# Four groups of VectorE instructions moved past the start of the next step in a fused state-space and mixture kernel

## The chip, the cores and the metric

The kernel runs on one core of a Trainium2 chip, in 32-bit floats throughout. The metric is the device time of one execution in microseconds (us).

## The reference, cut to what matters

A Mamba-2 state-space block is followed by a mixture of four experts, each a two-layer network on 3072 tokens of width 256:

```python
for c in range(S // 32):                       # per head, over chunks
    M = (C_c @ B_c.T) * L                      # L: causal decays
    y[c] = M @ x_c + (C_c @ state) * decay_to_i
    state = decay_full * state + (B_c * decay_from_j).T @ x_c
x = y.transpose(0, 2, 1, 3).reshape(3072, 256)
p = domain_probs / (domain_probs.sum(-1, keepdims=True) + 1e-9)
for e in range(4):                             # width 256 -> 1024 -> 256
    h = np.maximum(x @ w1[e], 0.0)
    out += p[:, e:e+1] * (h @ w2[e])
```

## The kernel before, in words

The tokens are cut into 24 chunks of 128. Six blocks (k = 0 to 5) of four chunks, 512 tokens each, go through the experts. For each block the experts' hidden width is cut into eight steps (r = 0 to 7, two for each expert), so there are 48 steps, n = 8k + r. Steps 0 and 1 are done in a plain way ahead of the loop; steps 2 to 47 are the loop of L718.

A step multiplies by Strassen's scheme in Winograd's form: seven products where eight would be needed, with sums before and after. A *first-layer product* i (`fmul(n, i)`, L436) is four matmuls of 256 columns; it writes or adds to one of two PSUM banks, X (products 1, 6, 7, 4) or Y (products 2, 5, 3). Products 1, 2 and 5 begin their bank anew, so product 5 may start only when the old Y has been read. ScalarE copies X after products 1, 6 and 7 (`snap`, L443), and VectorE adds the copy to Y (`total`, L448): the sums z11, z22, z12. From these, and from X directly, VectorE makes the gated activations h11, h22, h12, h21 (`gated`, L458), and from them four differences (`diff`, L465):

    T3 = h22 - h12,  T1 = h12 - h11,  T2 = h22 - T1,  T4 = h21 - T2

The seven *second-layer products* (`smul`, L521) of step n take these as their moving operand and are run inside step n+1, between that step's first-layer products. TensorE's order in the body of step n is: product 1, product 2, second-layer 1 of step n-1, product 6, second-layer 3, the attention outputs (`outputs`, L376 and L382, in some steps), products 5 and 7, second-layer 7 and 5, products 3 and 4, second-layer 6 (reads T2), 2, the scores of a chunk (`scores`, L353, in some steps), second-layer 4 (reads T4).

VectorE's order in the body of step n is: z11, h11, the first half of a chunk's decays (`decay_part`, a scan, L330), the transpose of the last block's output (`turned_out`, L610, where r = 1), z22, h22, the second half of the decays, z12, h21, h12, the masking of the scores (L363), T3, a short scan (L313), T1, T2, T4, the end of the last block's combination and the state updates.

The chunk of a later block enters (`c_in`) in steps with r = 0, 2, 4, 6 and leaves through `outputs` (`c_out`) in steps with r = 1, 3, 5, 7 of blocks 1 to 4; block 0 has r = 2, 4, 6 and 2, 3, 5, 7, and the last block has neither. After `outputs`, VectorE turns the chunk's contribution to the state, adds the decayed old state and spreads it for the next use (`carry`, L399, L401, L406). The state is used again one block later.

At the first step of a block (`ending`, r = 0) the four accumulators of the block before are combined into its output: part 0 on VectorE (L541), part 1 on GpSimd (four adds, L544 to L547), part 2 on VectorE (L549, L550, in block 0 L552 too).

All instructions are issued in the order in which the program states them, each engine running its own in that order; waits between engines are added where data or buffers need them. T2 and T4 have two buffers each, z three, the accumulators one each.

The end of the loop body, where the change is, is L793 to L801; its start is L732 to L737:

```python
        opened(n)                    # product 1, snap, product 2
        total(n, 1, "11")
        gated(n, "11", "z11")
        if c_in is not None:
            masks(c_in)
            decay_part(c_in, 0)
```

Of the kernel before, what the change touches and what calls it, by code (L numbers as in the profile page):

```python
# [17 lines left out]
def kernel(  # L18
# [101 lines left out]
    def load_chunk(c):  # L120
        load_tokens(c)
        load_decays(c, nc.sync)
# [3 lines left out]
    def load_w1(n):  # L126
        e, jj = divmod(n % SPB, JJ)
        t1 = wt1[n] = wts.tile([P, 7, HB], FP32, tag="wt1", name="wt1", bufs=5)
        if n >= SPB:
            nc.sync.dma_start(out=t1, in_=w1_d[n % SPB])  # L130
            return
        for k in range(2):
            nc.sync.dma_start(
                out=t1[:, 2 * k:2 * k + 2],
                in_=w1[e, k * P:k * P + P].rearrange("p (a f) -> p a f", a=2)[
                    :, :, jj * HB:jj * HB + HB])

    def load_w2(n):
        e, jj = divmod(n % SPB, JJ)
        t2 = wt2[n] = wts.tile([P, 7 * HB], FP32, tag="wt2", name="wt2", bufs=5)  # L140
        if n >= SPB:
            nc.sync.dma_start(out=t2, in_=w2_d[n % SPB])
            return
        for i in range(2):
            f = i * FH + jj * HB
            nc.sync.dma_start(
                out=t2[:, i * 2 * HB:(i + 1) * 2 * HB].rearrange("p (j m) -> p j m", j=JJ),
                in_=w2[e, f:f + HB].rearrange("(j p) m -> p j m", p=P))
# [17 lines left out]
    def sum_w1(n, part=None):  # L166


        if n < SPB:
            sums_of(lambda w: wt1[n][:, w].rearrange("p (j m) -> p j m", j=JJ), part)  # L170
            if part != 0:
                nc.gpsimd.dma_start(out=w1_d[n], in_=wt1[n])

    def sum_w2(n, part=None):
        if n < SPB:
            sums_of(lambda w: w2_op(n, w), part)
            if part != 0:
                nc.gpsimd.dma_start(out=w2_d[n], in_=wt2[n])
# [92 lines left out]
    def load_gate(k, e):  # L271
        g = gate[k, e] = ffn.tile([P, CPB, P], FP32, tag="gate", name="gate", bufs=3)
        nc.sync.dma_start(out=g, in_=p_d.rearrange(
            "(i k) e s -> k e i s", k=NBLK)[k, e].partition_broadcast(P))
# [64 lines left out]
    def masks(c):  # L339

        s = st[c]
        m = s["ctm"] = att.tile([HN, NT, P], FP32, tag="ctm", name="ctm")
        for t in range(NT):
            nc.scalar.mul(m[:, t], s["xb"][:, OCT:OCT + P], tmask[:, t:t + 1])
# [48 lines left out]
    def carry(c):  # L393
        s = st.pop(c)
        if "A" not in s:
            return

        S = att.tile([HN, D], FP32, tag="S", name="S", bufs=6)
        nc.vector.transpose(S, s["A"].rearrange("p t n -> p (t n)"))  # L399
        if c >= CPB:  # L400
            nc.vector.scalar_tensor_tensor(  # L401
                out=S, in0=state[c % CPB][0], scalar=s["dec"][:, P - 1:P], in1=S,
                op0=ALU.mult, op1=ALU.add)

        M = att.tile([HN, NQ, D], FP32, tag="M", name="M", bufs=6)
        nc.vector.tensor_mul(M, S.unsqueeze(1).to_broadcast([HN, NQ, D]), qmask)  # L406
        state[c % CPB] = S, M
# [37 lines left out]
    def total(n, i, b):  # L445

        z = first[n]["z" + b] = ffn.tile([P, JJ, HB], FP32, tag="z", name="z", bufs=3)
        nc.vector.tensor_add(z, first[n]["Y"], first[n][i])  # L448

    def gated(n, b, src):  # L450

        if n not in hid:
            hid[n] = {}
        h = hid[n][b] = ffn.tile([P, JJ, HB], FP32, tag="h" + b, name="h" + b)
        k, e = n // SPB, n % SPB // JJ
        half = int(b[1]) - 1
        g = gate[k, e].rearrange("p c s -> p (c s)")[:, half * HB:half * HB + HB]
        nc.vector.scalar_tensor_tensor(  # L458
            out=h, in0=first[n][src], scalar=0.0, in1=g.unsqueeze(1).to_broadcast([P, JJ, HB]),
            op0=ALU.max, op1=ALU.mult)  # L460

    def diff(n, o, x, y):
        h = hid[n]
        h[o] = ffn.tile([P, JJ, HB], FP32, tag="h" + o, name="h" + o)
        nc.vector.tensor_sub(h[o], h[x], h[y])  # L465
# [66 lines left out]
    def combine(k, part):  # L532

        p1, p3 = kept[k, 0][:, 0], kept[k, 0][:, 1]
        if part == 0:
            kept[k, "o"] = ffn.tile([P, 2, BLK], FP32, tag="o", name="o", bufs=1)
            kept[k, "u"] = ffn.tile([P, 3, HB], FP32, tag="u", name="u", bufs=1)
        o, u = kept[k, "o"], kept[k, "u"]
        b1, b2 = slice(0, HB), slice(HB, BLK)
        if part == 0:  # L540
            nc.vector.tensor_add(u[:, 0], acc[k, 2][:, 0], p1)  # L541
        if part == 1:
            p7, p5 = kept[k, 1][:, 0], kept[k, 1][:, 1]
            nc.gpsimd.tensor_add(u[:, 1], u[:, 0], p7)  # L544
            nc.gpsimd.tensor_add(u[:, 2], u[:, 0], p5)
            nc.gpsimd.tensor_add(o[:, 1, b2], u[:, 1], p5)
            nc.gpsimd.tensor_add(o[:, 0, b2], u[:, 2], p3)  # L547
        if part == 2:
            nc.vector.tensor_add(o[:, 0, b1], acc[k, 2][:, 1], p1)  # L549
            nc.vector.tensor_add(o[:, 1, b1], acc[k, 3][:, 0], u[:, 1])  # L550
            if k == 0 and PLAIN:
                nc.vector.tensor_add(o[:, 1, b2], acc[k, 3][:, 1], o[:, 1, b2])  # L552
# [69 lines left out]
    def opened(n):  # L622

        fmul(n, 1)
        snap(n, 1)
        fmul(n, 2)
# [88 lines left out]
    carry(1)  # L715


    for n in range(PLAIN, NS):  # L718
        k, r = divmod(n, SPB)

        enter, exit = ({2: 1, 4: 2, 6: 3}, {2: 0, 3: 1, 5: 2, 7: 3}) if k == 0 else (
            {0: 0, 2: 1, 4: 2, 6: 3}, {1: 0, 3: 1, 5: 2, 7: 3})
        c_in, c_out = (CPB * (k + 1) + d[r] if r in d and k < NBLK - 1 else None
                       for d in (enter, exit))
        ending = r == 0 and k > 0
        e = r // JJ
        if r % JJ == 0 and n + JJ < NS:
            load_gate(*divmod(n // JJ + 1, E))
        if PLAIN + 2 < n + 2 < NS:
            load_w1(n + 2)  # L730
            load_w2(n + 2)
        opened(n)  # L732
        total(n, 1, "11")
        gated(n, "11", "z11")
        if c_in is not None:
            masks(c_in)
            decay_part(c_in, 0)  # L737
        if n == PLAIN:
            for m in range(PLAIN):
                sum_w1(m, 1)  # L740
        elif n == PLAIN + 1:
            for m in range(1, PLAIN):
                sum_w2(m, 1)
        sum_w1(n + 2)
        if n > PLAIN:
            sum_w2(n + 1)
        if r == 1 and k > 0:
            turned_out(k - 1)
        if k > 0 and 1 <= r <= CPB:
            leave(k - 1, r - 1)  # L750
        smul(n - 1, 1)
        fmul(n, 6)
        snap(n, 6)
        smul(n - 1, 3)
        if ending:
            keep(k - 1, 0)
        if c_out is not None:
            outputs(c_out, ps_att, "att")
        fmul(n, 5)
        fmul(n, 7)  # L760
        snap(n, 7)
        total(n, 7, "22")
        smul(n - 1, 7)
        smul(n - 1, 5)
        if ending:
            keep(k - 1, 1)
        gated(n, "22", "z22")
        if c_in is not None:
            decay_part(c_in, 1)
        if n == PLAIN:  # L770
            sum_w2(0, 1)
        if c_out is not None and c_out + 2 < NCH:
            load_chunk(c_out + 2)
        fmul(n, 3)
        total(n, 6, "12")
        fmul(n, 4)
        gated(n, "21", "X")
        gated(n, "12", "z12")
        if r == SPB - 1 and k < NBLK - 1:
            sums(k + 1)  # L780
        smul(n - 1, 6)
        smul(n - 1, 2)
        if c_in is not None:
            scores(c_in, ((ps_att, "att"), (ps_att, "att"), (ps_f, "X"), (ps_f, "Y")))
            masked(c_in, (2, 3, 0, 1))
        diff(n, "T3", "22", "12")
        if c_in is not None:
            decay_part(c_in, 2)
        if ending:
            combine(k - 1, 0)  # L790
            combine(k - 1, 1)
        smul(n - 1, 4)
        diff(n, "T1", "12", "11")  # L793
        diff(n, "T2", "22", "T1")
        diff(n, "T4", "21", "T2")
        if ending:
            combine(k - 1, 2)
        if PLAIN < n <= CPB:
            carry(n - 1)
        if c_out is not None:  # L800
            carry(c_out)  # L801
    finish(NS - 1)


# [43 lines left out]
```

## Time and profile before

| | |
|---|---|
| time, median of three runs | 664.32 us (663.93 to 665.34) |
| the profiled execution's own time | 664.32 us |
| its span, first to last instruction | 662.5 us |
| TensorE matmul busy | 646.7 us, 98% |
| VectorE busy | 496.7 us, 75% |
| ScalarE, GpSimd busy | 115.0 us, 113.0 us (17% each) |
| mean granted TensorE clock | 0.999 of full speed |
| chain that ended last | TensorE 87%, VectorE 7%, DMA 4%, issue 1% |

Times are in microseconds from the first instruction. PE is TensorE's matmul stream, PEld its weight loads, which overlap it; DVE is VectorE, ACT ScalarE, POOL GpSimd, SP the engine that issues most transfers. In a row of the timeline the columns are start, duration, engine, line, operation, output and inputs; the bracket at the end is the time for which the engine stood idle before it and what released it. Several instructions of one kind in a row are merged into one with a count. Matmuls overlap one another in the pipeline: four of them are shown as 1.03 us, but follow each other group by group every 0.86 us.

### The profile page before, as it was taken

The page shows a single profiled execution, that of the slowest core. Times are in us where ns is not written, and L with a number is a line of the kernel's source. Part 1 is how long each engine was busy: PE and PEld are TensorE (multiplying, and loading weights), DVE is VectorE, ACT ScalarE, POOL GpSimd, SP SyncE. Part 2 cuts the span into 40 slices and gives each one's busy share as a digit, 9 for nine tenths or more (in the row PEclk, how much of TensorE's full clock was granted, in tenths as well). Part 3 has the DMA queues.
Part 4 walks back from the last instruction along what each step waited for, and adds up shares of the span by engine and source line. Part 5 has one row for each costly group of instructions (what it writes and reads, how often), then busy time and mean ns, then how long its engine had stood idle before and what let it go on. Part 6 is the DMA issues. An engine that isn't in the chain of part 4 may idle for free.

```text
span 662.5 us, 8905 instructions
## 1 busy us (share of the span) xinstructions
PE 646.7 (98%) x3359; PEld 541.2 (82%) x3359; DVE 496.7 (75%) x814; ACT 115.0 (17%) x246; POOL 113.0 (17%) x157
## 2 busy tenths in 40 slices
PE   8899989999999999999999999999999999999997
PEld 5687878878888887888887888888788888888886
DVE  8678788787786788767878777678867776856655
ACT  3011111221112122111122121112111112111110
POOL 4867483030000002000003000000200000200000
PEclk9999999999999999999999999999999999999999
DMA  7998998405669512868730566841265851176000
GB/s 228 318 335 326 344 371 312 171 2 171 207 257 330 186 56 65 251 192 290 279 131 3 195 208 255 323 169 56 75 242 191 307 220 62 19 244 242 5 1 32
DMA packets 68666, 127.09 MB, mean 192 GB/s; under 512 B 26616, under 2 KB 50576, under 8 KB 68624
## 3 DMA queue, kind: packets, MB, share of 16 engines
q1 hardware_dynamic: 65568, 111.32, 48.7%
q0 software_dynamic: 2304, 14.68, 5.4%
q8 instruction: 26, 0.43, 0.3%
q10 hardware_dynamic: 752, 0.54, 0.3%
q14 instruction: 16, 0.13, 0.1%
HBM read 108.44 MB, written 18.07 MB: 191 GB/s over the span
## 4 chain that ended last, share of the span: by engine, by line
PE 87%; DVE 7%; DMA 4%; issue 1%; SPq 0%; POOL 0%; ACT 0%; DVEq 0%; ACTq 0%; POOLq 0%
PE acc L521 40%; PE X L436 22%; PE Y L436 18%; DVE hT L465 3%; PE g L353 2%; PE acc L502 2%; PE y L382 1%; DVE MT L363 1%; DMA gate<-p_d 1%; PE y L376 1%; DMA ac_d<-a_sb 1%; DMA p_d<-p_sb 1%; DMA xb<-in_xbc_dram 1%; DVE z L448 1%; DMA wt<-w_d 1%
## 5 line engine op out<-in xcount | busy, mean ns | idle before, releaser
L521 PE MATMUL acc<-hT,wt 128*128 128x256 f32 x736 | 183.1, 382 | 0.0
L448 DVE TENSOR_TENSOR z<-Y,snap 128x512 f32<-128x512 f32 x138 | 94.6, 686 | 117.6 <-ACT snap L443 99.5
L443 ACT COPY snap<-X 128x512 f32<-128x512 f32 x138 | 80.8, 585 | 474.8 <-PE X L436 472.8
L521 PEld LDWEIGHTS acc<-hT,wt 128*128 128x128 f32 x736 | 138.3, 190 | 24.0 <-issue 6.0
L436 PE MATMUL X<-yS,wt 128*128 128x256 f32 x552 | 141.7, 379 | 0.0
L521 PE MATMUL acc<-h,wt 128*128 128x256 f32 x552 | 141.5, 379 | 0.0
L521 PEld LDWEIGHTS acc<-h,wt 128*128 128x128 f32 x552 | 104.9, 190 | 14.3
L436 PEld LDWEIGHTS X<-yS,wt 128*128 128x128 f32 x552 | 104.9, 190 | 14.3
L458 DVE SCALAR_TENSOR_TENSOR h<-z,gate 128x512 f32<-128x512 f32 x138 | 98.1, 711 | 3.5 <-PE acc L502 0.4
L436 PE MATMUL Y<-yT,wt 128*128 128x256 f32 x368 | 94.4, 379 | 0.0
L465 DVE TENSOR_TENSOR hT<-h,hT 128x512 f32<-128x512 f32 x92 | 75.8, 823 | 3.2
L436 PEld LDWEIGHTS Y<-yT,wt 128*128 128x128 f32 x368 | 68.8, 190 | 10.6
L465 DVE TENSOR_TENSOR hT<-h,h 128x512 f32<-128x512 f32 x92 | 64.4, 723 | 0.8
L436 PE MATMUL Y<-yS,wt 128*128 128x256 f32 x184 | 49.8, 393 | 6.8 <-DVE z L448 6.8
L330 DVE TENSOR_TENSOR_SCAN LT<-ab,ident 128x512 f32<-128x512 f32 x42 | 53.6, 1279 | 0.7 <-POOL wt L161 0.7
L335 POOL TENSOR_TENSOR MT<-xb,LT 128x128 f32<-128x128 f32 x20 | 8.5, 427 | 251.9 <-PE Y L436 133.8
L436 PE MATMUL X<-yT,wt 128*128 128x256 f32 x184 | 47.2, 379 | 0.0
L363 DVE TENSOR_TENSOR MT<-g,LT 128x256 f32<-128x256 f32 x96 | 34.0, 417 | 17.3 <-PE g L353 17.3
L436 PEld LDWEIGHTS Y<-yS,wt 128*128 128x128 f32 x184 | 32.9, 189 | 16.8 <-DVE z L448 10.3
L316 POOL TENSOR_TENSOR cts<-ctm,dec 128x256 f32<-128x256 f32 x20 | 18.5, 924 | 161.2 <-ACT snap L443 158.3
L458 DVE SCALAR_TENSOR_TENSOR h<-X,gate 128x512 f32<-128x512 f32 x50 | 34.3, 687 | 10.8 <-PE X L436 4.6
L436 PEld LDWEIGHTS X<-yT,wt 128*128 128x128 f32 x184 | 35.0, 190 | 4.8
(91 smaller groups left out, 340.3 us busy)
## 6 DMA issues: line engine op xcount, KB each, us to landing
wt<-w_d SPq DMA_DIRECT2D x80, 896.0 KB, 10.5
w_d<-wt POOLq DMA_DIRECT2D x16, 896.0 KB, 6.8
ab<-acut_d SPq DMA_DIRECT2D x21, 512.0 KB, 5.5
wt<-in_w_dram SPq DMA_DIRECT2D x32, 256.0 KB, 7.0
xb<-in_xbc_dram SPq DMA_DIRECT2D x24, 320.0 KB, 3.6
gate<-p_d SPq DMA_DIRECT2D x24, 256.0 KB, 9.3
out_dram<-ot SPq DMA_DIRECT2D x160, 16.0 KB, 5.0
ah<-ac_d SPq DMA_DIRECT2D x20, 64.0 KB
```

Of the source, the lines that this page charges most:

```text
L316: nc.gpsimd.tensor_mul(cts, s["ctm"], dec.unsqueeze(1).to_broadcast([HN, NT, P]))
L330: nc.vector.tensor_tensor_scan(out=LT[:, i * w:i * w + w], data0=s["a"][i], data1=ident.rearrange("p h s -> p (h s)")[:, :w], initial=0.0, ...
L335: nc.gpsimd.tensor_mul(s["MT"][:, :, P:], s["xb"][:, OB:OB + HN].rearrange("p (h n) -> p h n", h=NH), s["LT"][:, :, P - 1:P].to_broadcast( ...
L353: nc.tensor.matmul(out=g.rearrange("p t s -> p (t s)"), lhsT=s["xb"][k, OBT:OBT + P], rhs=s["ctm"][k].rearrange("p t s -> p (t s)"), start ...
L363: nc.vector.tensor_mul(s["MT"][:, h, 0:P], s["g"][q], s["LT"][:, h])
L436: nc.tensor.matmul(out=f[bank][:, j], lhsT=wt1[n][:, w, j * P:j * P + P], rhs=rhs, start=(i in (1, 2, 5) and j == 0), stop=(j == JJ - 1), ...
L443: nc.scalar.copy(out=s, in_=first[n]["X"])
L448: nc.vector.tensor_add(z, first[n]["Y"], first[n][i])
L458: nc.vector.scalar_tensor_tensor(out=h, in0=first[n][src], scalar=0.0, in1=g.unsqueeze(1).to_broadcast([P, JJ, HB]), op0=ALU.max, op1=ALU. ...
L465: nc.vector.tensor_sub(h[o], h[x], h[y])
L502: nc.tensor.matmul(out=acc[k, u][:, half], lhsT=w2_op(n, w)[:, j], rhs=hid[n][f"{i + 1}{b}"][:, j], start=(begins and i == 0 and j == 0), ...
L521: nc.tensor.matmul(out=acc[k, u][:, half], lhsT=w2_op(n, w)[:, j], rhs=rhs[:, j], start=(begins and j == 0), stop=(n % SPB == SPB - 1 and ...
```

## The change

At the end of a step, the differences T2 and T4, part 2 of the combination and the state updates are no longer issued. They are kept in a list, and the list is issued in the next step behind its z11 and h11 and ahead of its decays. After the last step the list is issued ahead of the final part.

```diff
+    late = []
     for n in range(PLAIN, NS):
...
         opened(n)
         total(n, 1, "11")
         gated(n, "11", "z11")
+        for work in late:
+            work()
         if c_in is not None:
             masks(c_in)
             decay_part(c_in, 0)
...
         smul(n - 1, 4)
         diff(n, "T1", "12", "11")
-        diff(n, "T2", "22", "T1")
-        diff(n, "T4", "21", "T2")
+        late = [lambda n=n: diff(n, "T2", "22", "T1"), lambda n=n: diff(n, "T4", "21", "T2")]
         if ending:
-            combine(k - 1, 2)
+            late.append(lambda k=k: combine(k - 1, 2))
         if PLAIN < n <= CPB:
-            carry(n - 1)
+            late.append(lambda n=n: carry(n - 1))
         if c_out is not None:
-            carry(c_out)
+            late.append(lambda c=c_out: carry(c))
+    for work in late:
+        work()
     finish(NS - 1)
```

## The prediction, made before the changed kernel ran

> **What bounds the kernel now.** I read the page first: busy times, then the costliest groups with the idle time in front of them.
>
> ```profile
> PE 646.7 (98%) x3359; PEld 541.2 (82%) x3359; DVE 496.7 (75%) x814; ACT 115.0 (17%) x246; POOL 113.0 (17%) x157
> L436 PE MATMUL Y<-yS,wt 128*128 128x256 f32 x184 | 49.8, 393 | 6.8 <-DVE z L448 6.8
> ```
>
> TensorE is busy for 646.7 of 662.5 us, so a change that leaves its work alone can only win idle time or lose more. Of the 15.8 us idle, 6.8 stand before one group, the matmuls that refill bank Y from yS: first-layer product 5. They wait for VectorE's z (L448), the sum z11, which must have read the old Y. The list of waits says "7 times, longest 1.4". The timeline gives the seven places: steps n=3 (0.65), 5 (1.24), 6 (0.43) and 9, 17, 25, 33 (1.37, 1.01, 1.01, 1.07). The timeline of both engines at the start of step 17, parts left out, shows what holds z11:
>
> ```profile
> 249.95 1.21 DVE L465 TENSOR_TENSOR hT<-h,h 128x512 f32<-128x512 f32 x1
> 251.19 2.23 DVE L465 TENSOR_TENSOR hT<-h,hT 128x512 f32<-128x512 f32 x2
> ...
> 253.03 0.70 PE L382 MATMUL y<-MT,xb 128*32 128x144 f32 x16
> ...
> 253.34 0.41 DVE L549 TENSOR_TENSOR o<-acc,kept 128x256 f32<-128x256 f32 x1
> 253.68 0.41 DVE L550 TENSOR_TENSOR o<-acc,u 128x256 f32<-128x256 f32 x1
> ...
> 254.01 0.68 DVE L448 TENSOR_TENSOR z<-Y,snap 128x512 f32<-128x512 f32 x1
> ...
> 254.72 0.69 DVE L458 SCALAR_TENSOR_TENSOR h<-z,gate 128x512 f32<-128x512 f32 x1
> ...
> 254.74 1.13 PE L436 MATMUL Y<-yS,wt 128*128 128x256 f32 x4 [1.01 <-DVE z L448]
> ...
> 255.33 1.24 DVE L610 STREAM_TRANSPOSE ot<-o 128x1024 f32<-128x1024 f32 x1
> ...
> 257.39 0.69 DVE L448 TENSOR_TENSOR z<-Y,snap 128x512 f32<-128x512 f32 x1 [0.82 <-ACT snap L443]
> ...
> 258.30 1.03 PE L436 MATMUL Y<-yT,wt 128*128 128x256 f32 x4
> ```
>
> VectorE never idles from T1 (249.95) to the output transpose: T2, T4 and the two combining adds stand ahead of z11, and nobody needs them so early (the second-layer products that read T2 and T4 come at the end of the step). The last two rows are the second thing to see. The next sum, z22 (257.39), is waited for by product 3 (258.30): z22 ends at 258.08, its weight load starts at once. So **z22 has no slack towards TensorE, and what VectorE has before it is a cushion of 0.82 us** (its idle time before z22). The moved instructions land exactly there. The question is thus in each step: gain at z11 against cushion at z22. An ordinary even step, n=18:
>
> ```profile
> 262.88 1.42 DVE L465 TENSOR_TENSOR hT<-h,hT 128x512 f32<-128x512 f32 x2
> ...
> 263.48 1.03 PE L436 MATMUL Y<-yT,wt 128*128 128x256 f32 x4
> ...
> 264.21 0.20 DVE L399 STREAM_TRANSPOSE S<-A 128x32 f32<-128x32 f32 x1
> ...
> 264.95 0.69 DVE L448 TENSOR_TENSOR z<-Y,snap 128x512 f32<-128x512 f32 x1
> ...
> 265.67 0.69 DVE L458 SCALAR_TENSOR_TENSOR h<-z,gate 128x512 f32<-128x512 f32 x1
> ...
> 266.28 1.22 DVE L330 TENSOR_TENSOR_SCAN LT<-ab,ident 128x512 f32<-128x512 f32 x1
> ...
> 269.47 0.69 DVE L448 TENSOR_TENSOR z<-Y,snap 128x512 f32<-128x512 f32 x1 [1.98 <-ACT snap L443]
> ```
>
> Here TensorE does not wait for z11 at all; the cushion is 1.98 us.
>
> **What the change moves.** No instruction is added or removed. T2, T4, the last combination (steps 9, 17, 25, 33, 41) and the state updates go from before z11, h11 to behind them. No DMA is among them; ACT, POOL and SP keep their order. Two effects.
>
> Gain at z11, the larger of what TensorE can recover. After attention outputs, product 5 follows 0.63 us after the start of the y group where nothing waits (280.38 to 281.01, step 19). Step 17 has 253.03 to 254.74, 1.71, so 1.08 too long; steps 25 and 33 likewise 1.08 and 1.14, step 9 (146.30 to 148.37) 1.44, step 3 (63.65 to 64.99) 0.71, step 5 (91.55 to 93.49) 1.31. Without outputs a product follows after 0.86: step 6 has 104.81 to 106.27, then 0.96 to the next, 0.70 in all. Steps 8, 16, 24, 32 lose 0.21 each that the idle column does not name (238.51, 239.47, 240.44, instead of 0.86 apart): 0.84. Together 1.44 + 1.08 + 1.08 + 1.14 + 0.71 + 1.31 + 0.70 + 0.84 = 8.3 us. That is the ceiling.
>
> Price at z22: the order up to z22 changes, the sum of VectorE's work does not, except for a bubble if T1 ends before z11 can start. z11 can start 1.13 us after product 2 starts (in the last block it waits for TensorE: product 2 at 603.22, z at 604.36).
> - Steps 9, 17, 25, 33: no bubble (product 2 of step 17 at 249.05, so z11 ready at 250.2, T1 done 251.16). The instructions from 251.19 to the transpose's end at 256.57 are the same; z22 then starts at 256.57 and not at 257.39, product 3 at about 257.32 and not 258.30, less 0.11 for TensorE's restart: 0.87. The gain is capped by the cushion: 4 x 0.87 = 3.5 instead of 4.74.
> - Step 3: product 2 at 59.67, z11 ready 60.80, T1 done 60.04: bubble 0.76, cushion 1.41, gain 0.65.
> - Step 5: no bubble, cushion 1.42, the whole 1.31. The wait of 0.64 us for cts (POOL) before it I leave as it is.
> - Step 6: bubble 0.33, cushion 0.84; T2 and T4, now 1.74 beside a POOL sum, run after that sum has ended (103.60) and cost 1.33: the whole 0.70.
> - Steps 8, 16, 24, 32: step 16 has product 2 at 235.92, z11 ready 237.05; then 0.72 (z) + 0.61 (h) + 1.33 (T2, T4) + 0.74 (state) + 1.14 (scan) = 4.54, to 241.59; z22 can start at 242.02. Margin 0.43: the whole 0.84.
> - Steps with r=2, 4, 6: step 18 has z11 ready 264.61, plus 4.54 is 269.15 against 269.47. Margin 0.32: nothing lost.
> - Step 4 has two state updates (1.18 for 0.74): 74.86 + 4.98 = 79.84 against 79.72, late 0.12, with restart 0.2 lost.
> - Odd steps without combination: T1 ends after z11 is ready (277.66 against 277.53 in step 19), so the order alone changes; cushion 2.82 intact: 0. The last block has cushions of 0.89 and more, and no such wait: step 41 has z11 ready at 568.09; two adds, 1.33 for T2 and T4 and the transpose end at about 572.7, before z22 at 572.96. 0.
>
> Sum: 3.5 + 0.65 + 1.31 + 0.70 + 0.84 - 0.2 = 6.8 us. The profiled execution took 664.32 us (span 662.5 and 1.8 around it), the same as the median of the three runs. 664.3 - 6.8 = 657.5.
>
> The unknown is the duration of the moved pair beside POOL. T2 and T4 take 0.67 apiece alone (1.33 in step 18), 1.1 beside POOL's combining adds (2.15 from 251.19 to 253.34). In the four combining steps h11 comes to lie beside those adds: it too has two SBUF inputs, and the line's instructions take 0.69 mostly, 1.26 at worst. If h11 takes 0.57 more and nothing is returned, 0.87 falls to 0.3: 2.3 us less. If T2 and T4 get past the adds and take 0.67, up to 0.82 comes back and the four give 4.7: 1.2 more. I take no change in the total, since the same amount of POOL work is overlapped either way. From this alone 656.3 to 659.8.
>
> One rule speaks against the move. The Trainium skill's page "SBUF — State Buffer", section "Who interferes with whom", says that a VectorE instruction with two SBUF inputs and a GpSimd instruction that reads SBUF exclude each other: the second to start blocks for the whole of the first; its summary advises placing whichever is off the critical path. The row shows less: two T instructions and the adds at 251.70 and 252.84 (1.17 each, 0.72 alone) run through at 1.1 apiece, where strict exclusion would need 0.67 + 0.72 = 1.39 a pair. By the rule the pair would be 0.63 longer (2.78 for 2.15) and the four steps would give 0.24 each: an estimate from that page, 660.0. I go by the row.
>
> **The rivals.**
> 1. All waits vanish and z22 is never late: 8.3 us, 656.0. For it: the margins of even steps; against: the cushion of 0.82 in the four largest steps.
> 2. The waits of the combining steps move from product 5 to product 3: h11 and the transpose keep VectorE full, and nothing of the 3.5 survives: 661.0. For it: VectorE is without idle time there from 249.95 to 256.57; against: it still had 0.82 left.
> 3. Slower: z22 becomes the bound in the even steps with one state update and a scan before it, n=8, 10, ... 32, thirteen of them, where the margin is 0.32 (0.43 with r=0). If T2 and T4 took 1.11 each there and not 0.67, z22 would be 0.56 late, with restart 0.67, thirteen times: 8.7 against 6.8 gained, 666.2. It decides where 13 such losses reach 6.8, 0.52 each: from about 0.73 us more work before z22 per step (0.52 + 0.32 - 0.11). Against it: POOL has no instruction between T1 and z22 in these steps, so nothing should stretch T2 and T4.
>
> **How the numbers follow.** The forecast's case gets 0.70, rival 1 0.09, rival 2 0.13, rival 3 0.06; 0.02 is left for a time unchanged. The range 655.2 to 661.6 holds the forecast with its unknown (656.3 to 659.8), rivals 1 and 2, and a run's spread of 0.6. No change means within 0.2% (1.3 us), which is about what a measurement of this kernel can tell. Faster, below 663.0: 0.89; same 0.05; slower 0.06.
>
> **What would show it.** Right: in the timeline, z11 directly behind T1 and the seven idle entries before product 5 gone; in steps 9, 17, 25, 33 a short wait before product 3 for z22, 0.1 to 0.5; VectorE's idle time before z22 in step 18 down from 1.98 to about 0.3, before step 19's still 2.8. TensorE's idle total falls to about 9. Wrong: T2 and T4 above 0.8 us in even steps, waits of product 3 for z22 there, or a new wait of the second-layer products for T2 or T4.

## The result, and the profile after

The changed kernel takes 660.24 us in the median (659.64 to 661.72, four runs), against 664.16 for the kernel before; the ratio is 0.9941, 95% interval 0.9920 to 0.9962. The forecast was 657.5, 2.7 us lower; the gain is 3.9 us where 6.7 were expected. The profiled execution took 659.85 us, with a span of 658.07, 4.5 less than before. TensorE's idle total fell from 15.8 to 12.4 us.

Two groups of the page of the changed kernel, with the idle time before them last:

```profile
L436 PE MATMUL Y<-yT,wt 128*128 128x256 f32 x368 | 95.0, 381 | 2.5 <-DVE z L448 2.4
L436 PE MATMUL Y<-yS,wt 128*128 128x256 f32 x184 | 49.3, 390 | 0.0
```

The 6.8 us before product 5 (Y<-yS) are gone entirely. A wait of 2.4 us stands before product 3 (Y<-yT), where there was none: the list of waits has it as four waits of 0.8 at most. The timeline at the start of step 17, VectorE up to z22 and GpSimd's four adds in full, TensorE where it counts:

```profile
246.77 1.22 DVE L465 TENSOR_TENSOR hT<-h,h 128x512 f32<-128x512 f32 x1
...
247.40 1.18 POOL L544 TENSOR_TENSOR u<-u,kept 128x256 f32<-128x256 f32 x1
...
247.91 0.68 DVE L448 TENSOR_TENSOR z<-Y,snap 128x512 f32<-128x512 f32 x1
...
248.53 0.72 POOL L545 TENSOR_TENSOR u<-u,kept 128x256 f32<-128x256 f32 x1
248.62 1.19 DVE L458 SCALAR_TENSOR_TENSOR h<-z,gate 128x512 f32<-128x512 f32 x1
...
249.22 1.18 POOL L546 TENSOR_TENSOR o<-u,kept 128x256 f32<-128x256 f32 x1
...
249.73 2.34 DVE L465 TENSOR_TENSOR hT<-h,hT 128x512 f32<-128x512 f32 x2
...
250.35 1.17 POOL L547 TENSOR_TENSOR o<-u,kept 128x256 f32<-128x256 f32 x1
250.48 1.13 PE L436 MATMUL Y<-yS,wt 128*128 128x256 f32 x4
...
252.00 0.41 DVE L549 TENSOR_TENSOR o<-acc,kept 128x256 f32<-128x256 f32 x1
...
252.33 0.41 DVE L550 TENSOR_TENSOR o<-acc,u 128x256 f32<-128x256 f32 x1
...
252.83 1.25 DVE L610 STREAM_TRANSPOSE ot<-o 128x1024 f32<-128x1024 f32 x1
254.00 0.65 DVE L448 TENSOR_TENSOR z<-Y,snap 128x512 f32<-128x512 f32 x1
...
254.71 1.13 PE L436 MATMUL Y<-yT,wt 128*128 128x256 f32 x4 [0.51 <-DVE z L448]
```

z11 now follows T1 directly and product 5 runs without a wait. But z22 (254.00) has no idle time before it any more, and TensorE waits for it. From the end of T1 to the end of the transpose VectorE needs 6.17 us (247.91 to 254.08); before, the same instructions in the other order needed 5.38 (251.19 to 256.57). h11 takes 1.19 beside GpSimd's adds.

In an ordinary even step, VectorE's row before z22 of step 18 is as forecast, the cushion down from 1.98 to a quarter of a microsecond, and TensorE does not notice:

```profile
265.99 0.69 DVE L448 TENSOR_TENSOR z<-Y,snap 128x512 f32<-128x512 f32 x1 [0.25 <-ACT snap L443]
```

The start of product 1 marks each step in the timeline; from mark to mark the steps of the two profiles took (us):

| step | before | after | gain, forecast | gain, measured |
|---|---|---|---|---|
| 3 | 14.06 | 13.34 | 0.65 | 0.72 |
| 4 | 12.93 | 13.70 | -0.20 | -0.77 |
| 5 | 15.56 | 13.45 | 1.31 | 2.11 |
| 6 | 13.62 | 13.25 | 0.70 | 0.37 |
| 8, 16, 24, 32 | 13.13 each | 12.93 each | 0.84 | 0.79 |
| 9 | 14.78 | 14.44 | 0.87 | 0.34 |
| 17, 25, 33 | 14.43 each | 14.12 each | 2.61 | 0.94 |
| 41 | 12.09 | 12.13 | 0 | -0.04 |
| all others | | | 0 | 0 |
| sum | | | 6.8 | 4.5 |

Steps 3 to 6 together gave 2.44 where 2.46 were forecast. In this profile nearly the whole shortfall lies in the four steps after a combination: 1.28 for 3.5.

### The profile page after: what moved, and what is told of

Same layout as the page of the kernel before. It is cut to its first block, busy times and chain, and to the rows that moved or that the text cites. A ratio compares the mean times of both kernels' runs of the same rounds, so it can differ in the third digit from the quotient of the medians.

```text
span 658.1 us, 8901 instructions
## 1 busy us (share of the span) xinstructions
PE 645.7 (98%) x3359; PEld 540.6 (82%) x3359; DVE 491.2 (75%) x814; ACT 115.0 (17%) x246; POOL 113.9 (17%) x157
## 5 line engine op out<-in xcount | busy, mean ns | idle before, releaser
L458 DVE SCALAR_TENSOR_TENSOR h<-z,gate 128x512 f32<-128x512 f32 x138 | 101.7, 737 | 3.5 <-PE acc L502 0.4
L465 DVE TENSOR_TENSOR hT<-h,hT 128x512 f32<-128x512 f32 x92 | 69.6, 757 | 1.6
L316 POOL TENSOR_TENSOR cts<-ctm,dec 128x256 f32<-128x256 f32 x20 | 18.5, 926 | 160.6 <-ACT snap L443 157.7
```

Of the source, the lines that this page charges most:

```text
L316: nc.gpsimd.tensor_mul(cts, s["ctm"], dec.unsqueeze(1).to_broadcast([HN, NT, P]))
L458: nc.vector.scalar_tensor_tensor(out=h, in0=first[n][src], scalar=0.0, in1=g.unsqueeze(1).to_broadcast([P, JJ, HB]), op0=ALU.max, op1=ALU. ...
```

## The experiments

Blocks 1 to 5 repeat from execution to execution to 0.02 us a step, so step lengths tell more than whole times. Block 0 and what comes before it do not repeat: the changed kernel profiled on a second chip took 70.09 us from step 3 to step 8 and not 67.08, with the same 508.24 from step 8 to step 47 (508.25 in the first profile; before 510.29).

**The changed kernel on the second chip.**

> The changed kernel once more, beside the others of this call, to have it on the same chip: about 4 us under the kernel before. Blocks 1 to 5, where the steps repeat to 0.01 us, are to show the same step lengths as in its first profile; block 0 may differ, since TensorE's wait for cts there hangs on when a weight load lands.

Ratio 0.9943 (0.9926 to 0.9961), median 661.84 beside 665.57 for the kernel before. Step lengths of blocks 1 to 5 as in the table. In block 0, step 3 again took 13.34, but steps 4, 5 and 6 took 12.96, 17.51 and 12.93 where the first profile has 13.70, 13.45 and 13.25: taken up below.

**State updates back in their place.** The edit, against the changed kernel:

```diff
-            late.append(lambda n=n: carry(n - 1))
+            carry(n - 1)
...
-            late.append(lambda c=c_out: carry(c))
+            carry(c_out)
```

> The state updates go back to their old place, before z11; T2, T4 and the end of the combination stay moved. Theory (bubble): behind T1, VectorE has nothing to do for 0.3 to 1.8 us in most even steps, and the state updates (0.74 us; 1.18 in step 4) fit there for nothing, so that z22 of step 4 and of step 6 is no longer late: steps 4 and 6 give back some 0.2 to 0.8 and 0.3 us, VectorE's idle time before z22 in ordinary even steps rises from 0.25 to about 1.0, nothing else moves: 659.0 to 659.7 against 660.2. Rival: the state updates before z11 are what TensorE waited for in step 3 (there beside a GpSimd sum, 2.06 us): the wait of 0.65 comes back and the kernel is at 660.5 or above.

Ratio 0.9937 (0.9912 to 0.9962), which the whole time can't tell from the changed kernel's. The steps can: z22 of step 18 has 0.98 us of idle time before it, not 0.25; step 3 stays at 13.34, so the rival's wait does not come back, and from step 8 to 47 it is 508.26, as with the updates moved. The state updates gain nothing by the move; their old place, in the time in which VectorE waits for product 2, is free: its idle time before z11 of step 18 goes from 1.77 to 1.03 and the step keeps its 12.93. Steps 4 and 6 take 12.93 and 12.97, which is no credit to this edit, since the changed kernel itself had 12.96 and 12.93 on the second chip.

**The end of the output behind h22.** The adds of L549 and L550 (in block 0 L552 too) and the transpose leave the stretch before z22, and with them the first of the output's transfers (`leave`):

```diff
-        if r == 1 and k > 0:
-            turned_out(k - 1)
-        if k > 0 and 1 <= r <= CPB:
+        if k > 0 and 2 <= r <= CPB:
             leave(k - 1, r - 1)
...
         gated(n, "22", "z22")
+        if r == 1 and k > 0:
+            combine(k - 1, 2)
+            turned_out(k - 1)
+            leave(k - 1, 0)
...
-        if ending:
-            late.append(lambda k=k: combine(k - 1, 2))
```

> In the steps behind a combination (9, 17, 25, 33, 41) the last two combining adds and the output transpose, 1.92 us of VectorE, go from before z22 to behind h22. Theory (place and port): z22 is late there because 6.1 us of work stand between T1 and it; without the 1.92 VectorE is free at about 252.0 in step 17, before z22's inputs at 253.5. The waits of product 3 (0.83, 0.51, 0.51, 0.56) and their restarts go: 2.8 us, to 657.4. Rival: what is put behind h22 makes z12 and h21 late, and products 1 and 2 of the next step wait: 660 or above.

Ratio 0.9907 (0.9890 to 0.9924). Steps 9, 17, 25 take 13.34 and 33 takes 13.29, which is what other steps with outputs take; from step 8 to 47 it is 504.74, 3.5 less than the changed kernel. The rival's waits of the next step do not appear. z22 of step 17 has cushion again:

```profile
254.01 0.69 DVE L448 TENSOR_TENSOR z<-Y,snap 128x512 f32<-128x512 f32 x1 [1.05 <-ACT snap L443]
```

This shows that the place before z22 is what costs; it does not tell whether the work there is too much, or too long because of GpSimd. Two runs went for that; both leave out the output's three-term sums, and so serve for times alone.

**No combining adds on GpSimd, first form.**

```diff
-            nc.gpsimd.tensor_add(u[:, 1], u[:, 0], p7)
...
+            nc.scalar.copy(out=u[:, 1], in_=u[:, 0])
+            nc.scalar.copy(out=o[:, 1, b2], in_=p5)
+            nc.scalar.copy(out=o[:, 0, b2], in_=p3)
```

> GpSimd's four combining adds are replaced by three copies on ScalarE, so the three-term sums of the output are left out; VectorE's order is that of the changed kernel. Theory (port): h11, T2 and T4 of steps 9, 17, 25, 33 are long only because GpSimd's adds run beside them. They fall to 0.69 and 1.33, T1 too, VectorE is ready for z22 at about 252.0 in step 17, the four waits go: 2.8 us, 657.4. Rival (place): the instructions are as long without them, z22 stays late by 0.5: 660.2.

Neither came: ratio 0.9971, steps 9, 17, 25 at 14.29. The copies, issued in step 16's body, stood in ScalarE's queue ahead of its copy of X after product 1 and waited for VectorE's first combining add; the copy of X came late, and four waits of 0.68 us before product 6 took the place of those before product 3. The run decided nothing on its question. T2 and T4 together did take 1.33 us in it. T1 did not fall with them: it took 1.21 still, beside GpSimd's cts (L316, 250.13 to 250.86), the product that the attention outputs' first matmuls read.

**Second form**, the copies issued at the start of step 17's list, behind that copy of X:

> As in the run without GpSimd's combining adds, but ScalarE's three copies, which stand in for them (the three-term sums of the output are left out), are issued behind its copy after product 1, so that they hold up nothing. Theory (port): h11 takes 0.6 and T2 with T4 1.33, the work from T1's end to the transpose's end falls from 6.1 to 4.6 us, z22 is in time and steps 9, 17, 25, 33 take the 13.34 us of other steps with outputs, not 14.44 and 14.12; the stretch from step 8 to 47 falls from 508.2 to 504.7. Rival (place): the same work with the transpose in front of z22 is late whatever GpSimd does; the steps stay at 14.1.

Ratio 0.9880 (0.9861 to 0.9900). Its VectorE rows at step 17:

```profile
248.06 0.68 DVE L448 TENSOR_TENSOR z<-Y,snap 128x512 f32<-128x512 f32 x1
...
248.77 0.69 DVE L458 SCALAR_TENSOR_TENSOR h<-z,gate 128x512 f32<-128x512 f32 x1
...
249.38 1.41 DVE L465 TENSOR_TENSOR hT<-h,hT 128x512 f32<-128x512 f32 x2
...
251.05 0.42 DVE L549 TENSOR_TENSOR o<-acc,u 128x256 f32<-128x256 f32 x1
...
251.55 1.25 DVE L609 STREAM_TRANSPOSE ot<-o 128x1024 f32<-128x1024 f32 x1
...
253.28 0.69 DVE L448 TENSOR_TENSOR z<-Y,snap 128x512 f32<-128x512 f32 x1 [0.48 <-ACT snap L443]
```

The order on VectorE is the changed kernel's, transpose in front of z22 included. h11 takes 0.69 and not 1.19, T2 and T4 1.33 from start to next start and not 2.27, VectorE is done with the transpose 4.74 us after z11's start and not 6.17, and z22 has 0.48 us to spare. (L549 and L609 of this kernel are L550 and L610 of the others.) Steps 9, 17, 25 take 13.34, the stretch from step 8 to 47 504.74, as the theory had it. So without GpSimd beside it the whole moved work fits before z22: the late z22 is due to the contention. One part of the longer work is not: the add in front of the transpose takes 0.50 here too (251.05 to 251.55).

**One more subtraction in the even steps.** It measures how much z22 may be late:

```diff
+    spare = const.tile([P, JJ, HB], FP32, name="spare")
...
+        if c_in is not None and k > 0:
+            nc.vector.tensor_sub(spare, hid[n]["11"], first[n]["z11"])
```

> One more 128x512 subtraction on VectorE, 0.67 us, into a tile that nothing reads, behind T2 and T4 in the sixteen even steps from 8 to 38 (those that take a chunk in). Theory (z22 without slack): its cushion of 0.25 us is used up in the thirteen of them with a state update, z22 is 0.42 late, with restart 0.53, thirteen times: 6.9 us, 667.1; the three in block 4 after step 32, with a cushion of 0.98, show nothing. Rival (average): VectorE is busy for 75% only and the subtraction is hidden: 660.2.

Ratio 0.9988 (0.9971 to 1.0006), median 664.85 beside 665.70: right in kind, wrong in size. Thirteen steps grew, from 12.93 to 13.11; the three in block 4 stayed at 12.93. But that is 2.4 us (510.63 for 508.25 from step 8 to 47), not 6.9. Step 18 on the timelines of VectorE and TensorE:

```profile
270.08 0.68 DVE L740 TENSOR_TENSOR spare<-h,z 128x512 f32<-128x512 f32 x1
270.69 1.22 DVE L330 TENSOR_TENSOR_SCAN LT<-ab,ident 128x512 f32<-128x512 f32 x1
...
271.82 0.66 DVE L448 TENSOR_TENSOR z<-Y,snap 128x512 f32<-128x512 f32 x1
```

```profile
270.73 1.89 PE L521 MATMUL acc<-hT,wt 128*128 128x256 f32 x8
272.54 1.13 PE L436 MATMUL Y<-yT,wt 128*128 128x256 f32 x4
```

z22 starts 0.28 late (its inputs would have let it start at about 271.54, 0.61 after ScalarE's copy at 270.93). Product 3 follows the eight matmuls after 1.81, which is 1.73 when nothing waits: 0.08 late, and 0.10 more until TensorE is back in its rhythm. So z22 has some 0.2 us of slack towards TensorE that the bracket before z22 does not show; the lead of the weight load seems to take it up: in step 18 of the changed kernel product 3's load begins at 266.74 and its matmuls at 266.90, here both begin at 272.54. That this lead is all of the slack was not tested.

**The output's end alone.** The kernel before, with only the end of the output moved behind h22:

> The kernel before with one thing moved: the last two combining adds and the output transpose behind h22 of the steps after a combination. T2, T4 and the state updates stay before z11. Theory (the end of the output is what is in the way in those steps): z11 of step 17 starts when T4 ends, 253.34 and not 254.01, product 5 waits 0.4 and not 1.0 us, z22 is in time; steps 17, 25, 33 take 13.75 instead of 14.43, the stretch from step 8 to 47 507 to 507.5 us, less than the changed kernel's 508.2; block 0 as before. Rival: T2 and T4 are what is in the way; the steps stay above 14.1 us.

Ratio 0.9945 (0.9925 to 0.9965), the changed kernel's own gain. Steps 17 and 25 take 13.77, the stretch from step 8 to 47 is 507.51, less than the changed kernel's 508.25. In these blocks, moving the end of the output alone, behind h22, is worth more than the change. It has a price in step 10, which takes 13.20 for 12.93: step 9, with its third add, ends late on VectorE, z11 of step 10 starts 3.74 us after its product 1 and not 2.33, and product 5 is late. With T2 and T4 behind z11 (the run on the end of the output, above), step 10 stays at 12.93.

**The kernel before, profiled again.**

> The kernel before, for its profile on the chip of this call. Blocks 1 to 5 should repeat the first profile (510.3 us from step 8 to 47); block 0 shows whether the first profile's 69.5 us from step 3 to 8 is the rule, or whether there too the wait for cts in step 5 is longer, as in three profiles of the changed order.

510.26 from step 8 to 47, 69.38 from step 3 to 8, step 5 15.42 with 0.50 of waiting for cts: as in the first profile.

**The helping edits together, and GpSimd's order.**

> The two runs that helped, together: state updates back before z11, end of the combination and transpose behind h22. Theory (the two act in different steps, so they add): steps 9, 17, 25, 33 at 13.34, step 4 at 12.9 and step 6 at 13.0 us, about 6.5 us under the kernel before. Rival: with the state updates back, TensorE waits for z11 again in step 3 or 6; no better than the later output alone.

Ratio 0.9881 (0.9860 to 0.9902), 656.72 beside 665.57. Steps 9, 17, 25 at 13.34, step 4 at 12.93, step 6 at 12.96; what is left is step 5, 15.51, with TensorE idle for 1.90 before the outputs, waiting for cts.

In block 0 GpSimd also makes and stores the sums of the expert weights that Strassen's scheme needs (L160 to L164). For the last run its weight sum `sum_w2(n + 1)` in steps with `c_in` is issued behind `decay_part(c_in, 2)`, which issues cts:

> The same, and GpSimd's sums of a second-layer weight in steps that take a chunk in are issued behind the chunk's cts, not before it. Theory: step 5's length (13.4 to 17.5 us in the runs so far) comes from cts queued on GpSimd behind two weight sums whose first waits for its load; with one of them behind cts, cts is done some 4 us earlier, step 5 takes 13.4 to 13.6, and the kernel gains 1 to 2 us more. Rival: the wait moves to the second-layer product that needs the summed weight: nothing gained.

Ratio 0.9852 (0.9834 to 0.9870), 654.79 beside 665.57, the best of all. Step 5 takes 13.34 and no wait turned up elsewhere; TensorE has no idle time from 45 us to the end of step 47. cts is done at 87.5 and product 5 of step 5 follows the outputs as anywhere. On the second chip the changed kernel's step 5 has, on GpSimd:

```profile
81.97 0.96 POOL L160 TENSOR_TENSOR wt<-wt 128x256 f32<-128x256 f32 x1 [9.12 <-DMA wt<-in_w_dram]
...
92.97 0.71 POOL L316 TENSOR_TENSOR cts<-ctm,dec 128x256 f32<-128x256 f32 x1
```

cts comes last in a queue of two weight sums and two stores, the first of which waits for its load. In the first profile of the changed kernel the first sum started at 78.22 and cts at 89.26, early enough. That first profile is the exception: with T2 and T4 moved and GpSimd's old order, the wait for cts in step 5 was 0 there, 0.31 in one run and 1.90 to 2.48 in the six others; with T2 and T4 in their old place it was 0.50 to 0.64 in three profiles.

## Why the prediction was right and where it failed

Right, with numbers: the seven waits before product 5 were due to T2, T4 and the rest ahead of z11, and all seven went. The steps with r = 0 gained 0.79 for 0.84, step 3 0.72 for 0.65. Ordinary even steps lost nothing, with a cushion of 0.25 where 0.32 was reckoned, odd steps and the last block moved by 0.04 at most. The mark to look for in steps 9, 17, 25, 33, a wait before product 3 "0.1 to 0.5", was there, but longer than said in all four: 0.83, 0.51, 0.51, 0.56. TensorE's idle total was to fall to about 9 and fell to 12.4.

The step that failed is one term: four times 0.87 for the steps after a combination. It was built on "The instructions from 251.19 to the transpose's end at 256.57 are the same", and on taking "no change in the total, since the same amount of POOL work is overlapped either way". The overlap did change: the work grew from 5.38 to 6.17 us. From start to next start, h11 took 1.11 for 0.61, T2 with T4 2.27 for 2.15, and the add in front of the transpose 0.50 for 0.33; the last has nothing to do with GpSimd, the transpose now directly follows the add whose output it reads. Of these 0.79 us, 0.11 came back because z11 starts as soon as T1 lets it, and some 0.1 because z22 and product 3 follow a little closer than reckoned: product 3 began 0.56 later in the step than forecast, and 0.87 less 0.56 is the 0.31 measured. Before, the adds ran beside T1, T2, T4, and the fourth beside z11, which they do not disturb. Now z11 comes early and h11, T2 and T4 meet the second, third and fourth. The lower end was in the prediction: h11 0.57 longer "and nothing is returned", 0.87 down to 0.3, and the total 659.8. Measured were 0.31 in three of the steps and 0.34 in the fourth. The four terms at 0.31 would have given a forecast of 659.7; that the value of no change was taken between two named ends is the mistake.

The rule weighed there and set aside was the better guide. The Trainium skill, page "SBUF — State Buffer", section "Who interferes with whom", says that a VectorE instruction with two SBUF inputs and a GpSimd instruction that reads SBUF exclude each other. The ends of the rows of step 17 fit such turns, one engine after the other: GpSimd's second add ends at 249.25, h11 at 249.81, the third add at 250.40, T2 at 250.94, the fourth add at 251.52, T4 at 252.08, each 0.54 to 0.59 behind the other engine's. The rows before show the same for T2 and T4 (251.74, 252.29, 252.87, 253.42). The prediction rejected the rule because whole durations, 0.67 and 0.72, would make 1.39 a pair; a turn is shorter than a duration, about 1.13 a pair. By turns the miss can be counted: before, T2 and T4 each waited out an add and z11, which does not wait, lay beside the fourth; now h11, T2 and T4 each wait one out. The estimate that the prediction drew from the rule, 0.24 a step and 660.0, is near the 0.31 measured by luck: it put T2 and T4 at 2.78 where 2.27 was measured, and nothing on h11.

Steps 4, 5 and 6 came out at -0.77, 2.11 and 0.37 for -0.2, 1.31 and 0.70, so right in sum only, and by luck. In both profiles of the changed kernel step 4's z22 is 0.12 late, as reckoned, but product 3 does not wait for it: on the second chip the step lost 0.03, not 0.2. In the first profile the weight load landed early, and GpSimd's sums came to lie beside h22 (1.25 us for 0.69) and h12 (1.61 for 0.78 on the second chip), so that the masking of the scores and the next step came late. The same early load ended the wait for cts in step 5 (0.64 before), which the prediction had left as it was. On the second chip step 6 gained the 0.70 forecast (0.69), and step 5 took 17.51: 2.32 of waiting for cts and, directly behind it, 3.4 us in which TensorE was granted half its clock. The gain of block 0, 2.4 us in the first profile, thus hangs on when a weight load lands, and was none in the second (70.09 us from step 3 to 8, for 69.52 and 69.38 before). What made the load late was not tried.

Of the rivals, the second (the waits of the combining steps move to product 3, 661.0) comes nearest: 2.2 of its 3.5 us. The third's price, 0.67 a step, was too high: z22 has some 0.2 us of slack that "no slack" denied, so its point of decision lies about as much higher.

## What to carry to other kernels

Work moved out of the way of one wait lands before the next one: count the idle time before the next waited-for instruction on the same engine, and then look at what other engines run beside the new place, since durations do not move along with the instructions. If an instruction sits between two waits and nobody needs it (here the output's transpose), move that first; it was worth as much alone as the whole change. In an engine with gaps, put the free work into the gap that is already there: the state updates cost nothing where they had been.

## What the runs showed of the hardware that was not expected

- VectorE's gated product (scalar_tensor_tensor with both tensors in SBUF) is stretched by GpSimd's adds as its plain subtractions are: 1.19 us for 0.69. The sum with one input in PSUM is not: z takes 0.651 to 0.693 in all 138 cases of the changed kernel. A GpSimd add beside h11, T2 or T4 takes 1.18, alone 0.72.
- In the second chip's profile of the changed kernel the granted TensorE clock was 1.00 from 33 us on but for a stretch of 3.4 us from 94.1, where it was 0.50; an earlier such stretch lies at 29.2 (0.51). In the one at 94.1 product 5's four matmuls took 2.01 us for 1.13. That stretch lies directly behind the 2.32 us of waiting for cts, and so do such stretches in two other runs with that wait; the second form without GpSimd's adds waited 2.48 without one, and its step 5 took 16.09, not 17.51. The first profiles of both kernels have no such stretch. Whole times of the changed kernel spread from 659.82 to 664.65 on the second chip, with these stretches and the wait for cts in the longest, where step lengths of blocks 1 to 5 agree to 0.02.
